# Retention attention with routed experts: every tile's scores as one product of 128 keys by 128 queries per head

## The chip, the cores and the metric

The kernel runs on one core of one Trainium2 chip. The metric is the device time of one execution in microseconds (us); lower is better. Times of this kernel below are medians of several runs. The rows of the profile come from one further execution, recorded by the hardware profiler.

## What is computed

The reference has two parts. The first is a retention layer: for each of 8 batches and 8 heads, 576 queries and keys of width 64, scores are scaled, multiplied by a decay that depends on the head and on the distance of query and key (zero for keys that come later than the query), and multiplied with V.

```python
scores = scale * np.matmul(q, k.transpose(0, 1, 3, 2))
gamma = 1.0 - 2.0 ** (-5.0 - np.arange(H, dtype=np.float32))
rel = pos[:, None] - pos[None, :]
Dmat = np.where(rel >= 0, gamma[:, None, None] ** rel[None, :, :], 0.0)
return np.matmul(scores * Dmat[None], v)
```

The second part takes the 4608 rows of 512 numbers that come out. Each row chooses one of 4 groups and one of 4 experts in that group, goes through that expert's two layers (512 to 1024, relu, 1024 to 512), and is weighted by the two softmax values of its choice. All inputs and outputs are 32-bit floats.

## The kernel before

**Tiles of the retention part.** The 4608 rows are cut into 36 tiles of 128 (`tiles`, line 311). For each pair of batches there are nine: four tiles of 128 positions from each batch (`m=0`), and one mixed tile (`m=1`) that holds the last 64 positions of both. The mixed tiles are 8, 17, 26 and 35.

**What one tile does on TensorE.** The decay between a query and a key is a product of two factors, one for each position. So the kernel scales V by the key's factor (`scale`, line 719, on ScalarE), and the result by the query's factor (`turned`, line 817, on VectorE). Between them stand plain products. `scores` (line 728) multiplies keys by queries inside the tile into `pss`, a PSUM tile of two banks: the first head of each pair in one bank (`o=0`), the second in the other (`o=1`). The two heads of a pair lie in partitions 0 to 63 and 64 to 127 of the same data. `masked` (line 755) reads `pss` on VectorE, one instruction per bank, multiplies by a mask of zeros and ones, and writes `sT`. `av` (line 786) multiplies `sT` with the scaled V into `px`. `state` (line 765) adds the tile's keys times values to a running sum for its batch, and `inter` (line 800) adds the queries times that sum of earlier tiles to `px`. A mixed tile updates no state; a first tile of a batch has no earlier state, so its `inter` issues nothing. Every 32-bit float product is issued as two instructions to TensorE, each with its own weight load.

**How scores are computed.** The first eight tiles (`FULL = 8`, line 35) issue eight products, one per head: 64 numbers deep, 128 keys as weights, 128 queries streamed. The other 28 tiles issue sixteen smaller ones (lines 742 to 753): the keys are cut into two halves of 64. The first half meets all 128 queries, the second half only the later 64, since earlier queries are masked for it; in a mixed tile each half meets only its own 64. The odd pairs of heads have their keys stored with the halves exchanged, so that four products that follow each other (two halves by two heads) fall on four different quarters of the TensorE array. What is not written in `pss` keeps older finite numbers and is masked to zero.

**Order of the work.** One loop (line 840) runs over the tiles, and each engine works strictly in the program's order. In step t TensorE does `av(t-1)`, `state(t)`, `inter(t-1)`, `scores(t+1)`, a transpose of an older tile (`xnat_pe`, line 356), and once in three steps the gate's products for a group of three tiles (`logits`, `gate_pe`, `places_pe`). VectorE does `choose` for a group, `turned(t-1)`, `weigh` and `masked(t+1)`. `pss` and `px` exist once, so `scores(t+1)` waits until `masked(t)` has read `pss`, and `av(t)` until `turned(t-1)` has read `px`. SyncE issues the loads of queries and keys (`a`) and of keys and values (`b`) six tiles ahead, into rings of seven buffers.

**The rest.** From step 31 on, the largest expert so far is picked (`pick`, line 514), its rows are read back from DRAM (`xload`, line 224), and its first layer starts inside the last step of the loop (`layer1`, line 559). Then 16 experts follow, each as 32-bit products split into a rounded part and a remainder, three products for one; TensorE's instructions for an expert's width stand twice, and a branch takes one of them (`by_width`, line 208).

Of the kernel before, what the change touches and what calls it, by code (L numbers as in the profile page):

```python
# [15 lines left out]
P = 128  # L16
RG = 3
B, H, S, D = 8, 8, 576, 64
# [3 lines left out]
NP = H // 2  # L22
# [9 lines left out]
LOADS = 7  # L32
WARM = 8

FULL = 8
NS = N + P
NT = N // P
NPIECE = 4
# [27 lines left out]
def moe_retention(ctx, tc, qk, kv, wgt, w1, w2, c_f, out):  # L66
# [55 lines left out]
    pe = nc.tensor  # L122
# [495 lines left out]
    with ExitStack() as ac:  # L618
# [4 lines left out]
        pss = ps_s.tile([P, 2, 4 * P], F32, name="pss")  # L623
# [104 lines left out]
        def scores(t):  # L728

            T = tiles[t]
            if t < FULL:
                for i in range(NP):
                    for o in range(2):
                        r = slice(o * D, o * D + D)
                        pe.matmul(  # L737
                            pss[:, o, i * P : i * P + P], T["kT"][r, i, :], T["qT"][r, i, :],
                            start=True, stop=True,
                        )  # L740
                return
            for i in range(0, NP, 2):
                for late in range(2):
                    for par in range(2):
                        for o in range(2):
                            k_ = slice((late ^ par) * D, (late ^ par) * D + D)
                            r = slice(o * D, o * D + D)
                            to = late * D + D if T["m"] else P
                            pe.matmul(  # L749
                                pss[k_, o, (i + par) * P + late * D : (i + par) * P + to],  # L750
                                T["kT"][r, i + par, k_], T["qT"][r, i + par, late * D : to],
                                start=True, stop=True,
                            )

        def masked(t):
            T = tiles[t]
# [79 lines left out]
        scale(0)  # L836
        first_gq()
        scores(0)
        masked(0)
        for t in range(NT + 1):  # L840
# [3 lines left out]
            r = t - PICK  # L844
# [26 lines left out]
            if t + 1 < NT:  # L871
                scores(t + 1)
                masked(t + 1)
# [601 lines left out]
```

## Time and profile before

| | us |
|---|---|
| median of 3 runs | 584.58 |
| lowest and highest of them | 583.65 and 586.3 |
| the profiled execution, as timed | 583.3 |
| its span, first to last instruction | 581.5 |
| TensorE matmuls busy in the span | 565.1 |
| VectorE busy | 424.1 |
| ScalarE busy | 325.9 |
| GpSimd busy | 258.0 |

Median and profiled execution lie 1.3 us apart, and 1.8 us of the profiled execution's time lie outside its span. The granted TensorE clock was 0.997 of full speed over the span. Of the profile's views the text uses the page, the waits, the stretches (busy time and instructions of each engine between two moments), the timeline (instructions in order of time, where neighbours of one kind are merged into one row: start, duration, engine, line, operation, operands, count), and the answer for one tile. PE is TensorE's matmuls, PEld its weight loads, DVE VectorE, ACT ScalarE, POOL GpSimd, SP SyncE and SPq its queue of transfers. Ends of matmuls are modelled and overlap the next one's start, so the text measures TensorE work from start to start. Instructions that go through the helper at line 117 all bear that line.

### The profile page before, as it was taken

What the parts mean: (1) busy time and instruction counts of PE and PEld (TensorE: products, weight loads), DVE (VectorE), ACT (ScalarE), POOL (GpSimd) and SP (SyncE); (2) the same over time, 40 slices, a digit from 0 to 9 for tenths busy, and PEclk for the clock granted to TensorE, in tenths of its full rate; (3) what the DMA queues carried; (4) which work ended last, traced back from release to release, by engine and by line L of the source; (5) the groups of instructions that cost most, each with busy time, mean ns of one, the idle gap of its engine ahead of it and who ended that gap; (6) DMA issues with size and microseconds to landing.
All of it is one profiled execution on the core that took longest, in us unless ns stands there. A gap on an engine that the chain in (4) does not pass through costs nothing.

```text
span 581.5 us, 16813 instructions
## 1 busy us (share of the span) xinstructions
PE 565.1 (97%) x6045; PEld 530.3 (91%) x6045; DVE 424.1 (73%) x997; ACT 325.9 (56%) x849; POOL 258.0 (44%) x391
## 2 busy tenths in 40 slices
PE   7998999999999999999999999999999999999995
PEld 4887788887779999999999999999999999999994
DVE  4886677878578768876767585767768687686774
ACT  5687878875456545454545454544545455455564
POOL 0022323334313047464555638273554835638455
PEclk9999999999999999999999999999999999999998
DMA  8998998966987943837476574929376594855841
GB/s 325 405 406 330 324 370 324 334 232 209 371 258 257 294 167 83 314 90 298 112 280 188 206 237 163 314 88 334 98 294 190 200 311 119 312 169 223 314 181 42
DMA packets 62410, 141.98 MB, mean 244 GB/s; under 512 B 9425, under 2 KB 30297, under 8 KB 62304
## 3 DMA queue, kind: packets, MB, share of 16 engines
q1 hardware_dynamic: 52944, 120.19, 58.9%
q0 software_dynamic: 9216, 20.28, 9.9%
q8 instruction: 73, 1.20, 0.8%
q14 instruction: 33, 0.27, 0.1%
q10 hardware_dynamic: 144, 0.05, 0.0%
HBM read 120.22 MB, written 24.81 MB: 249 GB/s over the span
## 4 chain that ended last, share of the span: by engine, by line
PE 85%; DVE 6%; DMA 2%; ACT 2%; issue 2%; SPq 1%; POOL 1%; POOLq 0%; ACTq 0%; DVEq 0%
PE ph L593 33%; PE py L998 11%; PE py L999 11%; PE py L1000 11%; PE px L793 4%; PE pss L749 2%; PE pxt L363 2%; PE px L811 2%; PE pst L778 2%; PE ph L579 2%; DVE sT L117 2%; PE py L987 1%; PE plt L405 1%; DMA xb<-xs 1%; DMA b<-in_kv 1%
## 5 line engine op out<-in xcount | busy, mean ns | idle before, releaser
L117 POOL DMA_INDIRECT out<-y,ii x151 | 165.2, 1094 | 64.0 <-issue 30.8
L117 DVE TENSOR_TENSOR wl<-r,wh 128x512 fp32r<-128x512 f32 x260 | 167.8, 687 | 5.9 <-ACT wh L117 2.4
L117 ACT ACTIVATE hh<-ph 128x256 fp32r<-128x256 f32 (+15 forms) x128 | 53.8, 421 | 203.1 <-PE ph L593 137.9
L117 ACT CAST wh<-r 128x512 fp32r<-128x512 f32 x260 | 147.0, 617 | 0.0
L593 PE MATMUL ph<-xTh_m,wh 128*128 128x324 f32 (+16 forms) x488 | 145.1, 297 | 0.0
L593 PE MATMUL ph<-xTl_m,wh 128*128 128x324 f32 (+16 forms) x488 | 144.4, 296 | 0.0
L593 PE MATMUL ph<-xTh_m,wl 128*128 128x324 f32 (+16 forms) x488 | 144.3, 296 | 0.0
L998 PE MATMUL py<-hh,wh 128*128 128x320 f32 (+19 forms) x480 | 143.2, 298 | 0.8 <-ACT hh L117 0.7
L1000 PE MATMUL py<-hl,wh 128*128 128x332 f32 (+14 forms) x480 | 141.8, 295 | 0.0
L999 PE MATMUL py<-hh,wl 128*128 128x332 f32 (+14 forms) x480 | 141.7, 295 | 0.0
L117 DVE SCALAR_TENSOR_TENSOR hl<-ph,hh 128x256 fp32r<-128x256 f32 (+14 forms) x122 | 56.6, 464 | 97.2 <-ACT hh L117 96.9
L593 PEld LDWEIGHTS ph<-xTl_m,wh 128*128 128x128 f32 x488 | 92.2, 189 | 0.5 <-issue 0.2
L593 PEld LDWEIGHTS ph<-xTh_m,wh 128*128 128x128 f32 x488 | 92.1, 189 | 0.4 <-issue 0.2
L593 PEld LDWEIGHTS ph<-xTh_m,wl 128*128 128x128 f32 x488 | 92.2, 189 | 0.0
L998 PEld LDWEIGHTS py<-hh,wh 128*128 128x128 f32 x480 | 90.5, 189 | 1.7 <-ACT hh L117 0.9
L999 PEld LDWEIGHTS py<-hh,wl 128*128 128x128 f32 x480 | 90.7, 189 | 0.0
L1000 PEld LDWEIGHTS py<-hl,wh 128*128 128x128 f32 x480 | 90.4, 188 | 0.0
L117 POOL COPY pace<-hh 1x1 f32<-1x1 f32 x140 | 31.1, 222 | 131.9 <-ACT hh L117 122.5
L117 POOL DMA_INDIRECT xs<-xt,sl x33 | 32.8, 993 | 104.4 <-DVE xT L117 37.3
L117 ACT ACTIVATE vs<-b,cf 128x64 f32<-128x64 f32 x288 | 72.4, 336 | 7.2 <-DMA b<-in_kv 5.9
L117 DVE TENSOR_TENSOR sT<-pss,masks 128x512 f32<-128x512 f32 x72 | 46.0, 681 | 12.0 <-PE pss L737 6.3
L793 PE MATMUL px<-sT,vs 128*64 128x128 f32 x576 | 39.4, 279 | 0.4 <-DVE xT L117 0.3
(194 smaller groups left out, 609.3 us busy)
## 6 DMA issues: line engine op xcount, KB each, us to landing
r<-in_w SPq DMA_DIRECT2D x138, 512.0 KB, 7.8
a<-in_qk SPq DMA_DIRECT2D x35, 512.0 KB, 6.6
b<-in_kv SPq DMA_DIRECT2D x31, 512.0 KB, 8.8
xb<-xs SPq DMA_DIRECT2D x20, 165.0 KB, 3.3
xb<-xs SPq DMA_DIRECT2D x20, 148.5 KB, 3.2
out<-y,ii POOLq DMA_INDIRECT x151, 3.0
xb<-xs SPq DMA_DIRECT2D x12, 181.5 KB, 4.8
b<-in_kv SPq DMA_DIRECT2D x6, 256.0 KB, 9.5
```

Of the source, the lines that this page charges most:

```text
L117: i_ = f(*a, **k)
L363: pe.transpose(T["pxt"][:, i, :], T["xT"][:, i, :], ident)
L405: pe.matmul(plt[32 * i : 32 * i + 32], wgp[:, i, :], tiles[t]["xTg"][:, i], start=True, stop=True)
L579: pe.matmul(ph[:, :C], raws[i][0][:, kc, cs], xTf[p][:, kc, :C], start=kc == 0, stop=kc == NKC - 1)
L593: pe.matmul(ph[:, :w], a[:, kc, cs], b[:, kc, :w], start=n == 0, stop=n == 3 * NKC - 1)
L749: pe.matmul(pss[k_, o, (i + par) * P + late * D : (i + par) * P + to], T["kT"][r, i + par, k_], T["qT"][r, i + par, late * D : to], start= ...
L778: pe.matmul(pst[o * D : o * D + D, i, :], T["k"][:, h, :], T["vs"][:, h, :], start=first and i == 0, stop=True, skip_group_check=True,)
L793: pe.matmul(px[g * D : g * D + D, o, s * P : s * P + P], T["vs"][:, 4 * s + 2 * g + o, :], T["sT"][:, o, 2 * s + g, :], start=s == 0, stop ...
L811: pe.matmul(px[g * D : g * D + D, o, s * P + r * w : s * P + r * w + w], st[rows, 2 * s + g, :], T["qT"][rows, 2 * s + g, r * w : r * w + ...
L998: pe.matmul(py[:, :w0], wh[:, f % 2, ds_], hh[:, :w0], start=st_, stop=False)
L999: pe.matmul(py[:, :w], wl[:, f % 2, ds_], hh[:, :w], start=False, stop=False)
L1000: pe.matmul(py[:, :w], wh[:, f % 2, ds_], hl[:, :w], start=False, stop=sp_)
```

## The change

The case distinction in `scores` goes, with the constant `FULL`. All 36 tiles, the mixed ones too, now issue the eight whole products that the first eight tiles issued before. Nothing else is edited: masks, `pss`, the loop's order and the loads stay as they were.

```diff
-FULL = 8
...
             T = tiles[t]
-            if t < FULL:
-                for i in range(NP):
-                    for o in range(2):
-                        r = slice(o * D, o * D + D)
-                        pe.matmul(
-                            pss[:, o, i * P : i * P + P], T["kT"][r, i, :], T["qT"][r, i, :],
-                            start=True, stop=True,
-                        )
-                return
-            for i in range(0, NP, 2):
-                for late in range(2):
-                    for par in range(2):
-                        for o in range(2):
-                            k_ = slice((late ^ par) * D, (late ^ par) * D + D)
-                            r = slice(o * D, o * D + D)
-                            to = late * D + D if T["m"] else P
-                            pe.matmul(
-                                pss[k_, o, (i + par) * P + late * D : (i + par) * P + to],
-                                T["kT"][r, i + par, k_], T["qT"][r, i + par, late * D : to],
-                                start=True, stop=True,
-                            )
+            for i in range(NP):
+                for o in range(2):
+                    r = slice(o * D, o * D + D)
+                    pe.matmul(
+                        pss[:, o, i * P : i * P + P], T["kT"][r, i, :], T["qT"][r, i, :],
+                        start=True, stop=True,
+                    )
```

## The prediction, made before the changed kernel ran

> **What bounds the kernel now.** I read the page first, for the busiest engine and the chain that ended last.
>
> ```profile
> PE 565.1 (97%) x6045; PEld 530.3 (91%) x6045; DVE 424.1 (73%) x997; ACT 325.9 (56%) x849; POOL 258.0 (44%) x391
> PE 85%; DVE 6%; DMA 2%; ACT 2%; issue 2%; SPq 1%; POOL 1%; POOLq 0%; ACTq 0%; DVEq 0%
> a<-in_qk SPq DMA_DIRECT2D x35, 512.0 KB, 6.6
> ```
>
> TensorE carries 85% of the chain. But this is an average over the retention tiles and the experts, and the edit touches only scores of tiles 8 to 35. So I asked for that tile's instructions and for the stretches around them (columns: stretch, its length, busy us and instructions of PE, PEld, DVE, ACT, POOL, granted clock, share of the 16 DMA engines, GB/s).
>
> ```profile
> L749 PE MATMUL pss<-a x896: 213/218/320, 33.3 to 137.6; 64*64 64x64 f32 x104, 64*64 64x128 f32 x76
> L737 PE MATMUL pss<-a x128: 272/272/373, 5.6 to 30.0; 64*128 64x128 f32 x128
> 15.00:30.00 15.00, 15.00 (x291) 12.70 (x287) 12.54 (x29) 9.88 (x40) 0.00 (x0) 1.00 1.03 406
> 33.25:137.10 103.85, 99.70 (x2321) 84.86 (x2317) 79.59 (x232) 81.88 (x285) 32.93 (x58) 1.00 0.86 317
> 200.00:569.00 369.00, 368.21 (x2775) 366.80 (x2774) 272.31 (x572) 187.47 (x409) 202.59 (x297) 1.00 0.61 212
> ```
>
> The small products (line 749) run from 33.3 to 137.6 us, the whole ones (line 737) before. In that stretch PE is busy for 99.7 of 103.85 us at full clock, VectorE for 79.6, ScalarE for 81.9. The waits from 30 to 142 us say what the rest is: first PE's, then one of PEld's and the longest of SyncE's queue (total us, times, longest).
>
> ```profile
> PE pst L778 <- issue: 1.7, 2, 1.2
> PE pss L749 <- issue: 1.4, 3, 0.7
> PE px L793 <- DVE xT L117: 0.3, 1, 0.3
> PE pxt L363 <- ACT vs L117: 0.3, 1, 0.3
> PEld pss L749 <- DVE sT L117: 0.9, 4, 0.2
> SPq L117 <- PE px L811: 61.7, 17, 7.7
> ```
>
> PE waits for data for little over 1 us. No wait is for a load: the loads wait for TensorE to free their buffers (61.7 us). So TensorE sets the pace here, and its instructions count one for one.
>
> **The products.** The first eight tiles are a sample of the new form, so I timed both forms in PE's timeline, from the start of `inter` (L811), or of `state` (L778) where `inter` is empty, to the start of what follows the scores. Whole products, first with, then without `inter`:
>
> ```profile
> 28.55 0.67 PE L811 MATMUL px<-a,st 64*64 64x128 f32 x16
> 29.15 1.16 PE L737 MATMUL pss<-a 64*128 64x128 f32 x16
> 30.24 0.66 PE L363 MATMUL pxt<-cf,xT 128*128 128x128 f32 x4
> 24.93 0.63 PE L778 MATMUL pst<-vs,b 128*64 128x64 f32 x16
> 25.49 1.16 PE L737 MATMUL pss<-a 64*128 64x128 f32 x16
> 26.59 0.55 PE L418 MATMUL pl<-cf,lt 128*128 128x128 f32 x3
> ```
>
> Small products: an ordinary tile, a mixed one, one without `inter`:
>
> ```profile
> 36.27 0.67 PE L811 MATMUL px<-a,st 64*64 64x128 f32 x16
> 36.76 0.85 PE L749 MATMUL pss<-a 64*64 64x128 f32 x32
> 37.54 0.66 PE L363 MATMUL pxt<-cf,xT 128*128 128x128 f32 x4
> 102.81 0.67 PE L811 MATMUL px<-a,st 64*64 64x128 f32 x16
> 103.29 0.64 PE L749 MATMUL pss<-a 64*64 64x64 f32 x32
> 103.87 0.66 PE L363 MATMUL pxt<-cf,xT 128*128 128x128 f32 x4
> 128.59 0.63 PE L778 MATMUL pst<-vs,b 128*64 128x64 f32 x16
> 129.16 0.90 PE L749 MATMUL pss<-a 64*64 64x128 f32 x32
> 129.99 0.66 PE L363 MATMUL pxt<-cf,xT 128*128 128x128 f32 x4
> ```
>
> Whole: 28.55 to 30.24 is 1.69 us; without `inter`, 24.93 to 26.59 is 1.66. Small: 1.27 ordinary, 1.06 mixed, 1.40 without `inter`. So a tile loses 0.42, 0.63 or 0.26 us. The scores alone go from 0.78 to 1.09; the other 0.11 of an ordinary tile lies between `inter` and the scores (0.49 to 0.60), where the form of the product now changes between two steps that had the same one. Of the 28 tiles 4 are mixed, 6 follow an empty `inter` (11, 15, 20, 24, 29, 33), 18 are ordinary: 18 x 0.42 + 6 x 0.26 + 4 x 0.63 = 7.6 + 1.6 + 2.5 = 11.6 us more on TensorE. That is why four small products side by side do better: they skip the masked quarter.
>
> **The stops for instructions.** Against it stands the count of instructions: per tile 16 MATMULs and 16 LDWEIGHTS fewer, 28 x 32 = 896 of the 4638 (2321 + 2317) in the stretch. The idle time called "issue" hangs on them. Six places in PE's timeline show it. Below are the first of them, then the first two and the last of the five stretches from stop to stop, then the last stop, which shows as a row drawn out to 1.36 us:
>
> ```profile
> 42.87 0.52 PE L778 MATMUL pst<-vs,b 128*64 128x64 f32 x12
> 44.58 0.34 PE L778 MATMUL pst<-vs,b 128*64 128x64 f32 x4 [1.19 <-issue]
> 44.84 0.90 PE L749 MATMUL pss<-a 64*64 64x128 f32 x32
> 44.57:50.54 5.97, 5.29 (x127) 4.15 (x126) 2.03 (x4) 4.12 (x15) 2.16 (x3) 1.00 0.99 380
> 50.54:68.40 17.86, 17.01 (x379) 14.96 (x380) 14.75 (x44) 13.89 (x48) 5.00 (x10) 1.00 0.90 318
> 96.26:118.20 21.94, 21.79 (x507) 18.52 (x506) 16.59 (x48) 17.88 (x63) 6.96 (x12) 1.00 0.91 329
> 117.77 1.36 PE L749 MATMUL pss<-a 64*64 64x128 f32 x32
> 119.05 0.66 PE L363 MATMUL pxt<-cf,xT 128*128 128x128 f32 x4
> ```
>
> From stop to stop TensorE gets 253, 759 and 1013 instructions: 1, 3 and 4 times 253. So a stop comes where a block of instructions ends, and about 18 blocks end in the stretch. `state` normally takes 0.56 us to the next start (24.93 to 25.49); at the first stop it takes 1.97, a loss of 1.41. At the last the scores take 1.28 for 0.78, a loss of 0.50. The six losses, worked out so, are 1.41, 0.95, 0.80, 0.72, 0.86 and 0.50: 5.2 us. Without them the 4638 instructions take 98.6 us, a block 5.4 us; the longest stop made that 6.8. From 15 to 30 us a block lasts 6.6 us (578 instructions in 15 us) and PE is busy all through, with the DMA engines as full (1.03). After the change 3742 instructions take 98.6 + 11.6 = 110.2 us, 7.5 us for a block. As the next block is then needed later than the slowest one came, all stops should go; bounds are 1.0 us (19% of 5.2, if stops only follow the count) and 5.2. I take 4.4, one of six left, since the stretch from 15 to 30 us is nearest in pace and load.
>
> The Trainium skill's page "Runtime: NRT & Kernel Launch" (Instruction fetch mechanics) says that an engine's instructions arrive in blocks of 256 and that crossing a block is mostly hidden. The row of 253 counted instructions agrees with the block; the 1.19 us does not agree with "hidden". By that rule alone nothing would be won at the blocks, and the sum would be 4.4 us higher.
>
> **Waits that the longer scores fill.** After step 31 the end is set by the readback of the first expert's rows:
>
> ```profile
> 135.00 1.09 PE L793 MATMUL px<-sT,vs 128*64 128x128 f32 x16 [0.32 <-DVE xT L117]
> 140.94 1.30 DVE L117 STREAM_TRANSPOSE xTf<-xb 128x512 f32<-128x512 f32 x2 [1.44 <-DMA xb<-xs]
> 142.30 1.99 PE L579 MATMUL ph<-xTf,r 128*128 128x256 f32 x8 [0.59 <-DVE xTf L117]
> ```
>
> VectorE waits for the transfer, TensorE for VectorE. Tiles 33 to 35 grow by 0.26 + 0.42 + 0.63 = 1.3 us, and 0.32 + 0.59 + 0.2 (one of the four waits for sT) = 1.1 of that fills waits. Bounds 0 and 1.3. The other waits for VectorE and ScalarE (0.7 + 0.3) shrink too; I take 0.6, between 0 and 1.0.
>
> **What costs nothing.** VectorE's mask instructions stay, two per tile; the longer scores lie ahead of `masked`, but `av` needs its result a step later. The loads of `a` on SyncE's queue go out later by what TensorE loses; they land in 6.6 us and are read about five steps of 3.7 us (103.85 / 28) after issue, so 12 us of cover remain. If the cover were gone, each late load would cost its lateness, and PE would show it.
>
> **Sum.** 11.6 - 4.4 - 1.1 - 0.6 = 5.5 us. The profiled execution took 583.3 us (span 581.5 and 1.8 around it), so 588.8; the median of the runs is 1.3 above that execution: 590.1 us, 0.9% slower. All reliefs at their largest (5.2 + 1.3 + 1.0) leave 4.1, none leaves 11.6.
>
> **Rivals.**
> *The stops stay.* They depend on what else the DMA engines carry, not on TensorE's pace. For it: only 6 of some 18 blocks stop. Against: none from 15 to 30 us. At a relief of 0 to 1 the sum is 8.9 to 9.9: 594 us.
> *Loads set the pace.* If queries arrive just in time, longer products fill time that TensorE would have waited. For it: DMA at 0.86 to 1.03. Against: SyncE waits 61.7 us for TensorE and TensorE never for a load. It decides only where PE waits for `a` or `b`. Time: no change to +1, 584.6 to 585.6.
> *Instructions set the price (faster).* An ordinary tile's 32 small MATMULs take 0.78 us, 24 ns each. If that is TensorE's price per instruction, and the 68 ns of a whole one (1.09 / 16) belong to the early stretch only, whole scores cost 16 x 24 ns = 0.39: 24 x 0.39 + 4 x 0.19 = 10.1 us less, and the stops go: 570 us. It decides from a pitch of whole scores below 0.78. Against: 32 of only 64 queries take 0.58, so length counts, and the clock was 1.00 in both stretches. The Trainium skill's page "TensorEngine Tiling (Array Packing)" (Instruction Overhead) gives each matmul a fixed cost, which would speak for this rival.
>
> **How the numbers follow.** Forecast, with its own range of 588 to 593 (from the 4.1 with all reliefs to a sum of 8 with half of the stops left): 0.62. Stops stay: 0.20. Loads set the pace: 0.13. Instructions set the price: 0.05. About 0.5% (2.9 us) is what a measurement can tell from no change; the line lies at 587.5. The forecast's low end is near it, and the three runs of before scatter by 2.7 us, so I count 0.04 of the 0.62 as no change. Slower: 0.58 + 0.20 = 0.78. Same: 0.13 + 0.04 = 0.17. Faster: 0.05. The range reaches down to 585.5, which leaves out the last rival and most of the third, and up to 596, near the sum without relief (584.6 + 11.6).
>
> **What would show it.** The changed profile should have 576 MATMULs of the whole form, 1.09 us from their start to the next; `inter` to scores 0.60; no or one "issue" stop between 33 and 148 us; the start of the first expert's layer some 5.5 us later than 142.30; the rest of the kernel moved by the same. A pitch under 0.8, or PE waiting for `a` or `b`, would make the prediction wrong; stops as many as before would put the time at 594.

## The result, and the profile after

The changed kernel takes 588.82 us (median of 10 runs, 587.93 to 590.12), the kernel before 585.81 us (median of 10, 582.05 to 588.42): ratio 1.0053, 95% interval 1.0028 to 1.0077. Timed again with nine runs, it took 589.31 against 585.69: 1.0061, 1.0040 to 1.0082. Two of the 14 runs of the kernel before in that series, 591.46 and 618.63 us, were slow and are left out of the ratio. So the changed kernel is slower by 3.0 to 3.6 us where 5.5 had been worked out. Its profiled execution took 589.1 us, 5.8 more than that of before. That one, with 583.3, was 2.5 quicker than its kernel's median, and the one of the changed kernel 0.3 slower than its own: 5.8 - 2.5 - 0.3 = 3.0.

The changed kernel's page, busy time and chain:

```profile
PE 575.5 (98%) x5597; PEld 537.1 (91%) x5597; DVE 424.9 (72%) x997; ACT 326.3 (56%) x849; POOL 258.4 (44%) x391
PE 88%; DMA 5%; DVE 3%; ACT 1%; issue 1%; POOL 1%; SPq 1%; POOLq 0%; ACTq 0%; DVEq 0%
```

TensorE has 448 MATMULs and 448 LDWEIGHTS fewer and is busy for 10.4 us more; VectorE's and ScalarE's shares of the chain have shrunk, and that of transfers (DMA) has grown from 2% to 5%. PE's timeline, with the start of tile 8's scores, an ordinary tile, a mixed one, the first pick's product (`pc`) and the first expert's first product:

```profile
33.76 1.16 PE L735 MATMUL pss<-a 64*128 64x128 f32 x16
85.15 0.67 PE L796 MATMUL px<-a,st 64*64 64x128 f32 x16
85.74 1.16 PE L735 MATMUL pss<-a 64*128 64x128 f32 x16
86.84 0.66 PE L362 MATMUL pxt<-cf,xT 128*128 128x128 f32 x4
105.05 0.67 PE L796 MATMUL px<-a,st 64*64 64x128 f32 x16
105.65 1.16 PE L735 MATMUL pss<-a 64*128 64x128 f32 x16
106.74 0.66 PE L362 MATMUL pxt<-cf,xT 128*128 128x128 f32 x4
132.13 0.18 PE L521 MATMUL pc<-ob,ones 128*128 128x16 bf16 x1
147.90 1.99 PE L578 MATMUL ph<-xTf,r 128*128 128x256 f32 x8 [1.12 <-DVE xTf L116]
```

From `inter` to what follows the scores is 1.69 us in both tiles, and the scores take 1.10 and 1.09, as predicted. From 30 to 148 us PE's waits are a single line; SyncE's queue still waits for TensorE, now for longer:

```profile
PE ph L578 <- DVE xTf L116: 1.1, 1, 1.1
SPq L116 <- PE px L796: 67.7, 19, 7.2
```

No "issue" line of PE is left, and none for a load.

From here on one stretch is the measure: from the start of tile 8's scores to the pick's product. It holds the scores of tiles 8 to 32 and leaves out how the kernel starts. In the changed kernel it is 132.13 - 33.76 = 98.37 us. In the kernel before, by these rows, it is 94.30:

```profile
33.25 0.69 PE L749 MATMUL pss<-a 64*64 64x64 f32 x32
127.55 0.18 PE L522 MATMUL pc<-ob,ones 128*128 128x16 bf16 x1
```

Of the 5.8 us between the two profiled executions 4.1 lie in this stretch, 0.5 ahead of it, 1.0 between the pick and the first expert (14.75 and 15.77 us), 0.2 behind.

### The profile page after: what moved, and what is told of

Same layout as the page of the kernel before. It is cut to its first block, busy times and chain, and to the rows that moved or that the text cites. A ratio compares the mean times of both kernels' runs of the same rounds, so it can differ in the third digit from the quotient of the medians.

```text
span 587.3 us, 15923 instructions
## 1 busy us (share of the span) xinstructions
PE 575.5 (98%) x5597; PEld 537.1 (91%) x5597; DVE 424.9 (72%) x997; ACT 326.3 (56%) x849; POOL 258.4 (44%) x391
## 4 chain that ended last, share of the span: by engine, by line
PE 88%; DMA 5%; DVE 3%; ACT 1%; issue 1%; POOL 1%; SPq 1%; POOLq 0%; ACTq 0%; DVEq 0%
PE ph L592 33%; PE py L983 11%; PE py L984 11%; PE py L985 11%; PE pss L735 5%; PE px L778 5%; PE pxt L362 3%; DMA b<-in_kv 3%; PE px L796 2%; PE pst L763 2%; DMA xb<-xs 2%; PE plt L404 1%; PE ph L578 1%; PE py L972 1%; POOL out L116 1%
## 5 line engine op out<-in xcount | busy, mean ns | idle before, releaser
L116 POOL COPY pace<-hh 1x1 f32<-1x1 f32 x140 | 32.8, 234 | 131.1 <-ACT hh L116 120.9
L735 PE MATMUL pss<-a 64*128 64x128 f32 x576 | 42.8, 289 | 2.1 <-DMA a<-in_qk 1.7
```

The source lines that it names most:

```text
L116: i_ = f(*a, **k)
L735: pe.matmul(pss[:, o, i * P : i * P + P], T["kT"][r, i, :], T["qT"][r, i, :], start=True, stop=True,)
```

## The experiments

Twelve runs. "Supply" stands below for the delivery of instructions to TensorE.

### Unchanged kernels once more

> The kernel before, unedited, profiled once more. Its times lie between 582.1 and 588.4 us, those of the changed kernel between 587.9 and 590.1. Theory: the stops for instructions differ from one execution to the next and make that scatter; the execution profiled first (583.3 us) had few of them, 5.2 us. So the loss at stops, counted in the same way between 30 and 140 us, should differ from 5.2 by about as much as the span differs from 581.5 us, with stops again at whole multiples of 253 instructions. Rival: the stops are the same and the span differs elsewhere (the readback at 138 us, the experts).

Measured on a chip on which the kernel before has a median of 592.44 us (23 runs), where the result above had 585.81. It took 591.79. PE's timeline:

```profile
34.33 0.69 PE L749 MATMUL pss<-a 64*64 64x64 f32 x32
49.93 1.43 PE L749 MATMUL pss<-a 64*64 64x128 f32 x32
51.28 0.66 PE L363 MATMUL pxt<-cf,xT 128*128 128x128 f32 x4
131.72 0.18 PE L522 MATMUL pc<-ob,ones 128*128 128x16 bf16 x1
```

The stretch is 97.39 us, 3.1 more. But the expectation held only in part: the small scores are drawn out in many places (here 1.35 us to the next start for 0.78), most of them not where a block ends. And of the 8.5 us by which the span is longer, 4.6 lie behind the start of the first expert, where the profile of this chip has ScalarE waiting for "issue".

> The kernel before, unedited, a third profile. Theory (supply): either few large stops at whole blocks (as at 581.5 us of span) or many drawn-out scores (as at 590.0); in both the loss against an undisturbed retention part explains when the first pick's product starts (127.6 and 131.7 us). Rival: the drawn-out scores of the second profile were an accident, and the pick's product is at 127 to 128 us again although the time is near 592.

This one took 586.92 us, on a chip where the kernel before has a median of 585.69. PE's timeline, and one stretch with the load of the DMA engines:

```profile
33.59 0.69 PE L749 MATMUL pss<-a 64*64 64x64 f32 x32
45.19 0.34 PE L778 MATMUL pst<-vs,b 128*64 128x64 f32 x4 [1.47 <-issue]
51.44 0.27 PE L749 MATMUL pss<-a 64*64 64x64 f32 x1 [0.96 <-issue]
86.87 0.56 PE L749 MATMUL pss<-a 64*64 64x128 f32 x14 [0.44 <-issue]
99.10 0.55 PE L749 MATMUL pss<-a 64*64 64x128 f32 x13 [0.99 <-issue]
130.30 0.18 PE L522 MATMUL pc<-ob,ones 128*128 128x16 bf16 x1
36.00:116.00 80.00, 74.08 (x1748) 63.62 (x1744) 57.76 (x162) 61.27 (x212) 23.73 (x43) 1.00 0.92 336
```

The stretch is 96.71 us. The stops stand before the same instructions as in the first profile (4 MATMULs of `state` left, 1, 14 and 13 of the scores), only longer: 1.47, 0.96, 0.44 and 0.99 us for 1.19, 0.69, 0.30 and 0.44. Not every block end stops in both, though: at 80.93 us stands a stop of 1.42 us, 1266 instructions (5 x 253) after the one at 51.44, where the first profile has none. So the places where a stop can come belong to the program; whether one comes, and how long it lasts, belongs to the execution.

> The changed kernel, unedited, timed and profiled once more beside the kernel before, to see whether the small difference holds where the kernel before is slow. The second profile of the kernel before (592 us) showed its small products drawn out: scores rows of 1.04 to 1.43 us where 0.85 is normal, not only where a block of instructions ends. Theory (supply): TensorE gets its instructions at a limited rate that differs between executions and chips; the changed kernel asks for fewer and doesn't feel it. Then it has no stops again, its retention part ends at the same 132 us (the first pick's product at 132.1), and where the kernel before is near 592 the two are within 0.5% of each other. Rival (the products alone decide): the changed kernel is slower by the same 3 to 6 us as where the kernel before took 585.8, ratio 1.005 to 1.010.

Same chip as the third profile of before; the ratio, 1.0061, is given above. The rows:

```profile
35.62 1.16 PE L735 MATMUL pss<-a 64*128 64x128 f32 x16
133.99 0.18 PE L521 MATMUL pc<-ob,ones 128*128 128x16 bf16 x1
```

The stretch is 98.37 us, the same to the hundredth as in the first profile, again without a stop. So this was not the chip with 592 us, and how the change does there was not measured.

### Half the loads, with small and with whole products

```diff
+            n = 2 if t < 8 else 1
...
-                    sp.dma_start(T[nm], src[nm][t])
+                    sp.dma_start(T[nm][:, 0:n], src[nm][t, :, 0:n])
...
-                T["qT"], T["kT"] = [T["a"][:, i].rearrange("p (i j) -> p i j", i=NP) for i in range(2)]
+                T["qT"], T["kT"] = [T["a"][:, i * (n - 1)].rearrange("p (i j) -> p i j", i=NP) for i in range(2)]
```

The same is done for `k` and `v`.

> The kernel before, but from tile 8 on only the queries are loaded (and used as keys too) and only the keys (used as values too); the loads of keys for the scores and of values are left out, which halves the traffic of the loads from 33 to 116 us. Only the retention part is compared, as other rows go to other experts. Theory A (instructions come late because their blocks queue behind the loads in the DMA engines): no stop left, small scores at 0.85 us everywhere, the first pick's product at 121 to 123 us against 127.6 and 131.7 in the two profiles of the kernel before. Theory B (TensorE's own intake of instructions is the limit, whatever the loads): the drawn-out scores stay, the pick's product at 127 to 132 us.

PE's timeline of this kernel, and a stretch:

```profile
34.41 0.69 PE L750 MATMUL pss<-a 64*64 64x64 f32 x32
84.97 0.85 PE L750 MATMUL pss<-a 64*64 64x128 f32 x32
85.75 0.66 PE L363 MATMUL pxt<-cf,xT 128*128 128x128 f32 x4
123.01 0.18 PE L522 MATMUL pc<-ob,ones 128*128 128x16 bf16 x1
36.00:116.00 80.00, 79.75 (x1901) 68.59 (x1895) 62.59 (x174) 67.38 (x234) 26.52 (x47) 1.00 0.70 226
```

Theory A holds. With the DMA engines at 0.70 instead of 0.92 PE is busy for 79.75 of 80 us instead of 74.08, no row of PE is marked "issue", and the stretch is 88.60 us. The products and their instructions are the same; only the loads differ. So the loads hold up the instructions, by 94.30 - 88.60 = 5.7 us in the first profile and 96.71 - 88.60 = 8.1 in the third. Step by step against this run, nearly all of both differences lies at block ends.

The blocks themselves are in the trace. The page lists a queue, q8, of kind "instruction"; below are its row before and after the change (packets, MB, share of the DMA engines), and a wait of the first profile that looks like another kind:

```profile
q8 instruction: 73, 1.20, 0.8%
q8 instruction: 69, 1.13, 0.8%
61.95 0.66 PE L363 MATMUL pxt<-cf,xT 128*128 128x128 f32 x4 [0.31 <-ACT vs L117]
```

Each packet of this queue is 16 KB, and 896 TensorE instructions fewer make 4 packets fewer. In the first profile each of the six stops ends 1.3 to 1.5 us after one of these packets has landed; for the first stop the packet lands at 43.13 us and TensorE goes on at 44.58. The wait at 61.95 us, put down to ScalarE, stands 1519 instructions (6 x 253) ahead of the stop at 96.27 and ends 1.5 us after a packet, and with half the loads it is gone. So it was a seventh stop. With half the loads the packets land about 1.9 to 3.1 us ahead of the same seven places, and TensorE doesn't stop. Whether a block is held up in the DMA engines or behind them, in memory, these runs don't tell.

> The changed kernel with the loads cut as in the run with half the loads: from tile 8 on queries serve as keys too and keys as values too, the loads of keys for the scores and of values are left out. With the small products that cut took the stretch from tile 8's scores to the first pick's product from 94.3 to 97.4 us down to 88.6. Theory (the loads hold instruction blocks up, and only the small products are quick enough to feel it): with whole products the stretch stays at the changed kernel's 98.4 us, within 0.5, so the products alone cost 98.4 - 88.6 = 9.8 us, against 10.3 from the prediction's rows for the 25 tiles in it. Rival (the loads slow TensorE's products themselves): the stretch gets shorter by 3 us or more here too.

```profile
34.15 1.16 PE L736 MATMUL pss<-a 64*128 64x128 f32 x16
132.52 0.18 PE L521 MATMUL pc<-ob,ones 128*128 128x16 bf16 x1
```

98.37 us, as with all loads. Whole products don't feel the loads, and the products alone cost 98.37 - 88.60 = 9.8 us. The whole times agree: 590.12 us against 580.82, both with half the loads (one run each, on two chips).

### Count or pace

```diff
+            if t >= 8:
+                for _ in range(16):
+                    pe.matmul(pss[:, 0, 0:1], ones, ones[:, 0:1], start=True, stop=True)
             for i in range(NP):
```

> The changed kernel, with 16 one-column bfloat16 products ahead of the scores of each tile from 8 on, whose result the scores overwrite: 32 instructions per tile, so the count is that of the kernel before, at the changed kernel's pace. Theory (pace): a product of this kind takes about 27 ns from start to start, so 0.43 us a tile, 12 us in all; 253 instructions last 6.6 us, as from 15 to 30 us, where nothing stopped: no stop, or one short one. Some 600 us. Rival (count): about six stops as in the kernel before, 5 us more, 606 us.

It took 609.08 us, on the chip with 592. PE's timeline:

```profile
33.81 0.54 PE L734 MATMUL pss<-ones 128*128 128x1 bf16 x16
43.46 0.34 PE L799 MATMUL px<-a,st 64*64 64x64 f32 x3 [0.44 <-issue]
84.93 0.21 PE L799 MATMUL px<-a,st 64*64 64x64 f32 x1 [0.50 <-issue]
147.23 0.18 PE L521 MATMUL pc<-ob,ones 128*128 128x16 bf16 x1
```

The stretch is 113.42 us, 15.05 more than 98.37. Sixteen tiny products take 0.48 us in 22 of the 25 tiles, near the 0.43 expected, or 12.0 us in all. Of the other 3 us, 2.1 lie in the `inter` of the three mixed tiles, which is a double one (64 instructions in about half a microsecond): it takes 1.24 to 1.39 us to the next start, against 0.62 or 0.63 in the changed kernel. Two of the three show as rows marked "issue". The rest is in a few drawn-out rows. So there was more than the one short stop of the pace theory and less than the 5 us of the rival. On the same chip, with as many instructions, the kernel before lost 97.39 - 88.60 = 8.8 us, so the count alone doesn't bring the stops back. But the run separates count from pace only in part: as it takes longer, its loads are thinner too (a DMA share of 0.81 from 36 to 116 us, against 0.93).

### Small products in some tiles only

```diff
-            if t < FULL:
+            if t < FULL or not T["m"]:
```

> The changed kernel, but the four mixed tiles keep the small products. Theory (products count one for one, stops for instructions come only where a block of 253 is used up in less than about 6.8 us): three mixed tiles win 0.63 us each against the changed kernel, the fourth (tile 35) hides behind the readback; no stops, as only 128 instructions come back. So 1.9 us under the changed kernel's 588.8: 586.9, beside 585.8 of the kernel before, ratio 1.002. Rival (stops hit any block by chance, whatever the pace): one or two stops in 15 blocks, 587.5 to 588.5.

Median 593.06 us (12 runs) beside 592.44 of the kernel before: ratio 1.0003, 0.9977 to 1.0029. PE's timeline:

```profile
33.39 0.69 PE L749 MATMUL pss<-a 64*64 64x64 f32 x32
41.59 0.34 PE L811 MATMUL px<-a,st 64*64 64x64 f32 x3 [0.41 <-issue]
113.67 0.21 PE L811 MATMUL px<-a,st 64*64 64x64 f32 x1 [0.45 <-issue]
132.10 0.18 PE L522 MATMUL pc<-ob,ones 128*128 128x16 bf16 x1
```

A miss: the stretch is 98.71 us, not 1.9 under 98.37, the stretch of the changed kernel on the other chips. What three mixed tiles win, 1.7 us, is lost again two steps later, at the double `inter`: 1.37, 1.18 and 1.34 us to the next start for 0.62 or 0.63, 2.0 us more. The four profiles from this chip all have such stops, those from the others none. The next kernel is the same line with `not (T["m"] or t % 2)`.

> Small products in the mixed tiles and in the twelve odd ordinary tiles from 9 on, whole ones in the others. Theory: against the changed kernel the products win 8 x 0.42 + 4 x 0.26 + 4 x 0.63 = 6.9 us, of which 0.9 (tiles 33 and 35) hides behind the readback; blocks last about 6.4 us on average, so at most two short stops. 588.8 - 6.0 = 582.8, to 584 with two stops; ratio to the kernel before about 0.995 to 0.997, faster than both kernels. Rival (stops follow the count of instructions): 4254 of 4638 instructions in the stretch, so most stops are back, 4 to 5 us of them: 587, ratio 1.002.

Median 592.41 us, ratio 1.0007, 0.9985 to 1.0028; the stretch is 132.07 - 34.51 = 97.56 us by PE's rows:

```profile
34.51 0.69 PE L749 MATMUL pss<-a 64*64 64x64 f32 x32
132.07 0.18 PE L522 MATMUL pc<-ob,ones 128*128 128x16 bf16 x1
```

Also a miss, and nearer to the rival's number: half of the tiles small won less than 1 us. The double `inter` of three tiles took back 2.0 us, and six rows of small scores, drawn out to between 0.94 and 1.29 us for 0.78, another 2.5. That the supply does this is likely but not shown, as no run with half the loads was made on this chip. Since the kernel before takes longer on this chip too, the two can't say what the same mixture does on the other chips.

### What the price of a whole product hangs on

```diff
+            q0 = D if t >= 8 else 0
...
-                        pss[:, o, i * P : i * P + P], T["kT"][r, i, :], T["qT"][r, i, :],
+                        pss[:, o, i * P + q0 : i * P + P], T["kT"][r, i, :], T["qT"][r, i, q0:P],
```

> The changed kernel, but from tile 8 on the whole products stream only the later 64 of the 128 queries; the scores of the earlier 64 queries are left out. The count of instructions stays that of the changed kernel. Theory (TensorE's products count one for one as long as the supply of instructions holds): the scores fall from 1.09 to about 0.55 us from start to start; 25 tiles before the first pick's product bring it from 132.1 to about 119, at 460 instructions per group of three tiles in about 10.4 us, 44 per us; few stops. Rival (VectorE, ScalarE or the loads are next): the pick's product stays above 124 us, and PE waits for sT, xT, vs or loads.

```profile
92.73 1.11 PE L736 MATMUL pss<-a 64*128 64x64 f32 x16
93.77 0.66 PE L362 MATMUL pxt<-cf,xT 128*128 128x128 f32 x4
```

Neither theory: half the queries take 1.04 us where all take 1.09, the stretch is 130.60 - 33.57 = 97.03 us, and PE waits for nothing. At these sizes the price of a whole product is hardly set by the queries it streams; what sets it, no run shows.

```diff
-                            to = late * D + D if T["m"] else P
...
-                                pss[k_, o, (i + par) * P + late * D : (i + par) * P + to],
-                                T["kT"][r, i + par, k_], T["qT"][r, i + par, late * D : to],
+                                pss[k_, o, (i + par) * P : (i + par) * P + P],
+                                T["kT"][r, i + par, k_], T["qT"][r, i + par, :],
```

> The kernel before with its small products, but from tile 8 on each half of the keys meets all 128 queries, so nothing of the masked quarter is skipped. Whole products of only 64 queries took 1.04 us for 16 MATMULs, hardly less than with 128 (1.09), so the number of queries isn't what a whole product costs. Theory (the small form is faster because four weight loads of 64 keys go side by side, not because it skips a quarter): the scores without skipping stay well under 1.09 us from start to start where nothing stops, 0.8 to 0.95 against 0.78 with skipping. Rival (the skipped quarter is the gain, as the prediction put it): 1.05 to 1.1 us, as long as the whole products.

```profile
33.25 1.10 PE L748 MATMUL pss<-a 64*64 64x128 f32 x32
84.94 1.05 PE L748 MATMUL pss<-a 64*64 64x128 f32 x32
85.93 0.66 PE L363 MATMUL pxt<-cf,xT 128*128 128x128 f32 x4
129.42 0.18 PE L522 MATMUL pc<-ob,ones 128*128 128x16 bf16 x1
```

Between the two: 0.99 us without skipping, 0.78 with, 1.09 whole. Of the 0.31 us that small scores win, 0.21 come from the skipped quarter and 0.10 from the form. It took 584.87 us (one run, beside a median of 585.65): as quick as the kernel before, though its scores take 0.2 us longer in each ordinary tile of the stretch and 0.4 in each mixed one, some 5.6 us in all. Its stretch is 96.17 us, and only two rows of PE are marked "issue" (0.92 and 0.55 us): slower products and fewer stops, as the balance would have it, in one execution.

The Trainium skill's page "TensorEngine Tiling (Array Packing)" (Tiling Modes) counts two tiles of 64x128 and four of 64x64 that work side by side; as an estimate from that alone, 8 x 128 / 2 and 16 x 128 / 4 columns, both forms would cost the same without skipping. The runs show 1.09 and 0.99.

### Loads from another queue

```diff
+                q_ = act if nm == "b" and t >= LOADS - 1 else sp
...
-                    sp.dma_start(T[nm], src[nm][t])
+                    q_.dma_start(T[nm], src[nm][t])
```

> The kernel before, but from tile 6 on the loads of keys and values (b) are issued from ScalarE's queue and no longer behind the loads of queries on SyncE's. All bytes are loaded. Each load then starts when its own buffer is free, half a step apart, where both started together before. Theory: an instruction block then waits behind less, the stops shrink, and the stretch from tile 8's scores to the first pick's product falls from 94 to 97 us toward 88.6: 91 to 93, the time by 3 to 5 us, to some 581 to 583 where the kernel before takes 585.7, and faster than both kernels. Rival 1 (what counts is the traffic as a whole, not its spacing): the same stretch of 94 to 97 us, ratio within 0.3% of 1. Rival 2 (the issue costs ScalarE time that TensorE waits for): slower by 1 to 5 us, with PE waiting for vs or xt.

Median 587.27 us (12 runs) against 585.65: ratio 1.0033, 1.0004 to 1.0062. PE's timeline of the profiled execution (585.32 us):

```profile
14.28 0.98 PE L779 MATMUL pst<-vs,b 128*64 128x64 f32 x16 [3.63 <-ACT st L117]
37.07 0.69 PE L750 MATMUL pss<-a 64*64 64x64 f32 x32
129.87 0.18 PE L522 MATMUL pc<-ob,ones 128*128 128x16 bf16 x1
```

The stretch is 92.80 us, the shortest with all loads, as the theory wanted. But TensorE waits 3.63 us for ScalarE at 14 us, tile 8 starts 3.8 us later, and the kernel is 1.6 us slower, not 3 to 5 faster; in time rival 2 comes nearest. One execution, with three rows of PE still marked "issue" (at 58.77, 87.28 and 98.78 us), doesn't show that the spacing shortened them.

> The same move of the b loads in the changed kernel, as a control. It has no stops to lose. Theory: the stretch stays at 98.4 us and the time at the changed kernel's, 1.005 to 1.006 of the kernel before. Rival (the move helps or costs by itself): it differs from that by more than 2 us in the same direction as the move in the kernel before.

Median 591.66 us (6 runs), ratio 1.0103, 1.0061 to 1.0146, over 2 us more than the changed kernel on the other chips (588.82 and 589.31).

```profile
37.01 1.16 PE L736 MATMUL pss<-a 64*128 64x128 f32 x16
135.38 0.18 PE L521 MATMUL pc<-ob,ones 128*128 128x16 bf16 x1
```

98.37 us a fourth time, so the theory had the stretch right; in the time the rival was right, since the move costs its late start in both kernels. Whether it saves stops stays open. No version tried here that computes everything measurably beats the kernel before.

## Why the prediction was right, and where its sum was off

The direction and the mechanism were right: more work for TensorE in the products, less lost at stops for instructions, the first larger than the second. That 5.5 us came so near the 5.8 between the two profiled executions was partly luck. In the stretch the prediction's terms make 10.3 - 4.4 - 0.6 = 5.3 us and 4.1 was measured; outside it they make 1.3 - 1.1 = 0.2 and 1.7 was measured. Point by point:

- *The products.* 11.6 us for 28 tiles, of which 17 x 0.42 + 5 x 0.26 + 3 x 0.63 = 10.3 lie in the stretch. Measured with half the loads, where nothing else differs: 9.8. The 0.5 between them lies in three steps of `state` that took up to 0.17 us longer before small scores; they are short waits of the kind for which 0.6 was taken.
- *Why they cost more.* "They skip the masked quarter" was two thirds of it: 0.21 of 0.31 us; the rest is the form.
- *The stops.* They vanish with whole products, all of them, in each of four profiles. But this is the term of the sum that was mis-sized: "4.4 us", with "bounds ... 1.0 us ... and 5.2". Both ends came from one execution, and a seventh stop was counted as a wait for ScalarE (0.3 us). By the stretch the loss is 5.7 us in that execution and 8.1 in another of the same kernel. The three stretches of before are 94.30, 96.71 and 97.39 us where the changed kernel has 98.37 each time, so the difference is 4.1 or 1.7 us, and 1.0 if the stretch is the same on the chip with 592; the medians moved by 3.0 and 3.6. It fits the scatter: the runs of the kernel before lie 6.4 us apart, those of the changed one 2.2.
- *From execution to median.* The last step added the 1.3 us between the profiled execution and the median of before, 588.8 to 590.1. The changed kernel's median is 588.82. Where one execution of the kernel before is longer than another, the stops are a part of it (2.4 of the 3.6 us between the spans of its first and third profile lie in the stretch). The changed kernel has none, so it had no reason to be 1.3 us above its own profiled execution.
- *What makes a stop.* The prediction gave the pace of TensorE, and left open what else the DMA engines carry, as a rival. It takes both: at the small products' pace half the loads end the stops, and with all loads whole products end them, at fewer instructions per microsecond (35 in the stretch, against 48 with half the loads and small products).
- *The readback.* Tiles 33 to 35 were to disappear in waits. From the pick to the first expert are 14.75 us before and 15.77 after in the first pair of profiles, 14.99 and 14.86 in the pair from one chip (and 14.44 in the profile at 592 us). The second pair shows the growth of 1.3 us hidden; in the first the transfer of `xb` itself took 4.70 us against 2.71.
- *The loads.* Their cover held: PE waits for no load after tile 8 in any profile of the changed kernel.

The rivals fell with these runs: stops that stay (none in four profiles), loads that set the pace (98.37 us with all and with half of them), instructions that set the price (1.09 us a tile all along).

Of the rule that crossing a block of instructions is mostly hidden (the Trainium skill, "Runtime: NRT & Kernel Launch", Instruction fetch mechanics) the runs show both sides: hidden at a DMA share of 0.70, not at 0.92 to 0.94 with the small products' pace.

Three things stay open: what sets the price of a whole product, what draws out the small scores on the chip with 592 us outside the ends of blocks (of the 8.8 us by which its stretch exceeds 88.60, some 6 lie there), and what the change does to the time on that chip.

## What to carry to other kernels

A product that is split to skip work costs instructions, and here these came as 16 KB packets through a DMA queue beside the loads. Where loads keep the DMA engines busy (here over 0.9), count instructions per microsecond beside products, and look for idle time marked "issue" at even distances; a wait put down to another engine can be one of them. Before a small loss or gain is sized from a profile, take the lost term from several executions; here it ran from 5.7 to 8.1 us while the work itself repeated to the hundredth. A sample of the new form that already runs in the old kernel, as the first eight tiles did, prices an edit well.

## What the runs showed of the hardware that was not expected

- Sixteen MATMULs of whole products took 1.04 us with 64 queries and 1.09 with 128; the 32 of the small form took 0.58, 0.78 and 0.99 us with 64, on average 96, and 128 queries. The small form pays by the query, the whole one hardly.
- A stop for instructions ended 1.3 to 1.5 us after a 16 KB packet had landed, at seven block ends of the first profile; with half the loads the packets landed 1.9 us or more ahead of the same places.
- With whole products and no stops the stretch repeated exactly: 98.37 us in four executions of three kernels, at DMA shares from 0.66 to 0.93 between 36 and 116 us.
- Chips differ in the same program: medians of 585.65, 585.69 and 592.44 us on three of them for the kernel before.
